# Sketch matrices as first loads, longer dummy matmuls, token-ordered q with interleaved projections, and a causal mask on row pairs

## The chip, the cores and the metric

The kernel runs on one core of one Trainium2 chip. The metric is the device time of one execution in microseconds (us), lower is better. TensorE (PE, with its weight loads as PEld), VectorE (DVE), ScalarE (ACT), GpSimd (POOL) and SyncE (SP) each run their own list of instructions in order; SP, and ACT in part, also issue the DMA transfers. They wait for one another through semaphores only.

## The reference

Two blocks follow each other. The first is a polynomial-sketch attention over 4 batches, 4 heads, 1088 tokens and 32 features; the second is a mixture of 4 attention experts, of which each token uses the best 2. S1 and S2 arrive as float64, all else as float32.

```
def phi(x):
    a = einsum('rd,bhsd->bhsr', S1, x)            # r = 8
    b = einsum('rd,bhsd->bhsr', S2, x)
    return einsum('bhsi,bhsj->bhsij', a, b)       # 64 features
q_p, k_p = phi(q), phi(k)
kv = einsum('bhsf,bhsd->bhfd', k_p, v);  z = k_p summed over tokens
x = (q_p @ kv) / (q_p @ z + 1e-6)                 # (B, S, H*D) = (4, 1088, 128)

logits = x @ w_gate;  topk = best 2 of 4;  w = softmax over those 2
for e in range(4):
    scores = (x @ wq[e]) @ (x @ wk[e]).T / 8, causal mask, softmax
    out += (weight of e, 0 if not chosen) * (softmax @ (x @ wv[e]) @ wo[e])
```

## The kernel before, in words

Nearly all of the work is matmuls and transposes on PE. PE's order is written out by hand (`manual_schedule`); a scheduler orders the other engines. Tokens lie in 9 tiles of 128 (the last has 64).

**Start.** SP loads k, then S1, q and v of batch 0 (`load`, L84); ACT loads wq, S2, wk, wv, w_gate and wo (L184 to L188). DVE turns the raw bits of S1 and S2 into float32 pairs (hi and lo, L128 to L147, some 20 small instructions), transposes them (`ST`, L153), and the block-diagonal sketch matrix `SKW` is filled from that by two copies on DVE and two on POOL (L155). Beforehand PE multiplies the identity with itself 10 times without use (`warm`, L552). Every float32 matmul has two records in the trace, and a float32 transpose one.

**prepare(b)** makes what the experts need of batch b: `begin` (L208) transposes k and q on DVE in 32x32 blocks; `sketch` (L220) multiplies with `SKW` (`kps`, `qps`), adds the lo part and forms the 64 products a feature row (`kp`, `qp`; DVE for batch 0, POOL later); `kvs` (L247) sums kv; `turn_features` (L263, `tq`) transposes qp; `numer` (L274, `num`) multiplies with kv, divides (`den`, `xs`); `turn_x` (L291, `tx`) transposes x into `xT`; `project` (L302, `qk`) makes q and k of the experts, `project_v` (L313, `vg`) v and the gate's logits, `gate` (L319) picks the two experts. q lies in the order in which its rows were loaded (34 tokens a partition), so `turn_x` puts its copy out of PSUM into token order with a stride of 34 elements.

For batch 0 the pieces run one after the other, and the projections of the first 1024 columns come when all of x is there. For batches 1 to 3 the same pieces are fillers: `spend` (L468) puts one between the units of the batch before, by a share of the costs that stand beside the pieces (L342 to L362).

**Units.** A unit is one tile of 128 queries and a pair of experts. `scores` (L367) multiplies on half of PE's rows each (64 features an expert: expert e on rows 64e to 64e+63, `sc`), adds the causal mask to the last 128 columns by a matmul of a 128x128 bfloat16 identity with a mask (L382, one per expert, on all 128 rows), DVE takes the maximum (L386, L389), ACT the exponential (L365). The scores are transposed (`tp`, L434), multiplied with v (`av`, L497) and wo (`po`, L540). There are 16 units a batch, 64 in all, and a last unit of 64 queries a batch (`scores_last`, L393) whose mask is at L412. `evacuate` (L67) copies PSUM to SBUF on ACT, each third time on DVE. PSUM has four buffers `tp` for all but the scores.

```
for e in range(2):
    nc.tensor.matmul(sc[e][:, 128 * i : n], identb, cmask, start=False, stop=True)
```

Of the kernel before, what the change touches and what calls it, by code (L numbers as in the profile page):

```python
# [19 lines left out]
def kernel(  # L20
# [20 lines left out]
    nc = tc.nc  # L41
# [59 lines left out]
    nc.vector.memset(raw, 0.0 if NS == 1 else 0)  # L101
    for x, s in enumerate((S1, S2)):
        eng = (nc.sync, nc.scalar)[x]
        if NS == 1:
            eng.dma_start(out=raw[R * x : R * x + R], in_=s)
        else:
            eng.dma_start(out=raw[R * x : R * x + R].rearrange("p d w -> p (d w)"), in_=s.bitcast(I32))
    load(0)
    if NS == 2:
# [34 lines left out]
        both(last, last, ok, ALU.mult)  # L144
# [23 lines left out]
    identb = const("identb", [128, 128], BF16)  # L168
    nc.vector.tensor_copy(identb, ident)
    cmask = const("cmask", [128, 128], BF16)  # L170
    make_causal_mask(nc, cmask, mask_val=-1e30)
# [8 lines left out]
    wqk = const("wqk", [128, 2, E, HD])  # L180
    wvg = const("wvg", [128, E * HD + E])
    wo_sb = const("wo", [128, NG, DM])
    for x, w in enumerate((wq, wk)):
        nc.scalar.dma_start(out=wqk[:, x], in_=w.rearrange("e p d -> p e d"))  # L184
    nc.scalar.dma_start(
        out=wvg[:, 0 : E * HD].rearrange("p (e d) -> p e d", e=E), in_=wv.rearrange("e p d -> p e d"))
    nc.scalar.dma_start(out=wvg[:, E * HD :], in_=w_gate)
    nc.scalar.dma_start(out=wo_sb, in_=wo.rearrange("(g e) h d -> (e h) g d", g=NG))  # L188

    nc.vector.tensor_scalar_mul(wqk[:, 0], wqk[:, 0], scale)  # L190


    def prepare(b):
# [13 lines left out]

        def begin():  # L208
# [3 lines left out]
            with tc.issue_after(mark[0]) if b < 2 else nullcontext():  # L212
# [3 lines left out]
                nc.vector.transpose(qT[:, 0:S], qin)  # L216
# [57 lines left out]
        def numer(g):  # L274
            num = bank(f"num{b}_{g}")
            for y in range(6):
                nc.tensor.matmul(num[:, 66 * y : 66 * y + 66], qpT[:, 6 * g + y],  # L277
                                 kvz[:, y % 2].rearrange("p h d -> p (h d)"), start=True, stop=True)
            nu = num[:, 0 : 12 * (D + 1)].rearrange("p (m d) -> p m d", d=D + 1)
            den = p2.tile([128, 12], F32, tag="den", name=f"den{b}_{g}")  # L280
            xs = p2.tile([128, 3, 128], F32, tag="xs", name=f"xs{b}_{g}", bufs=3)
            nc.vector.tensor_scalar_add(den, nu[:, :, D], 1e-6)
            nc.vector.reciprocal(den, den)
            last = nc.vector.tensor_tensor(
                out=xs.rearrange("p x (h d) -> p (x h) d", d=D), in0=nu[:, :, 0:D],
                in1=den[:, :, None].to_broadcast([128, 12, D]), op=ALU.mult)
            if first:
                mark[:] = [last.ins]
            xss[g] = xs

        def turn_x(g):  # L291
            tx = bank(f"tx{b}_{g}")
            for x in range(3):
                nc.tensor.transpose(tx[:, 128 * x : 128 * x + 128], xss[g][:, x], ident)
            c0, c1 = 12 * g, min(12 * g + 12, C)
            evacuate(xT.rearrange("p (t c) -> p c t", c=C)[:, c0:c1, :],
                     tx[:, 0 : 32 * (c1 - c0)].rearrange("p (c t) -> p c t", t=32))
# [21 lines left out]
        def gate():  # L319

            lg = vt[:, :, E * HD :]
            mine = lg[:, :, :, None].to_broadcast([128, NJ, E, E])
            theirs = lg[:, :, None, :].to_broadcast([128, NJ, E, E])
            gt = p2.tile([128, NJ, E, E], F32, tag="gt", name=f"gt{b}")
            eq = p2.tile([128, NJ, E, E], F32, tag="eq", name=f"eq{b}")
            rank = p2.tile([128, NJ, E], F32, tag="rank", name=f"rank{b}")
            top = p2.tile([128, NJ], F32, tag="top", name=f"top{b}")
            nc.vector.tensor_tensor(out=gt, in0=theirs, in1=mine, op=ALU.is_gt)
            nc.vector.tensor_tensor(out=eq, in0=theirs, in1=mine, op=ALU.is_equal)
            nc.vector.tensor_tensor(out=eq, in0=eq, in1=lower[:, None].to_broadcast([128, NJ, E, E]), op=ALU.mult)  # L330
# [3 lines left out]
            nc.vector.tensor_tensor(out=gw, in0=lg, in1=top[:, :, None].to_broadcast([128, NJ, E]), op=ALU.subtract)  # L334
            nc.scalar.activation(out=gw, in_=gw, func=ACTF.Exp)
            nc.vector.scalar_tensor_tensor(out=gw, in0=rank, scalar=2.0, in1=gw, op0=ALU.is_lt, op1=ALU.mult)
            nc.vector.reduce_sum(top, gw, axis=AX.X)
            nc.vector.tensor_scalar_add(top, top, 1e-9)
            nc.vector.reciprocal(top, top)
            nc.vector.tensor_tensor(out=gw, in0=gw, in1=top[:, :, None].to_broadcast([128, NJ, E]), op=ALU.mult)  # L340
            for g in range(NG):
                nc.vector.tensor_copy(gw8[64 * g : 64 * g + 64], gw[0:64, NJ - 1, 2 * g : 2 * g + 2])  # L342
# [309 lines left out]
```

## Time and profile before

| what | us |
|---|---|
| three runs: lowest, median, highest | 418.72, 419.71, 420.01 |
| the profiled execution, its own time | 420.57 |
| its span in the trace, first to last instruction | 418.7 |
| PE busy | 396.7 (95%) |
| DVE, ACT, POOL busy | 232.1, 224.9, 55.9 |

The profiled execution's span is 1.9 us shorter than its time, and its time is 0.9 us above the median of the runs. Busy PE time is not PE at its peak: matmul records overlap. A record's "us" in a timeline is from its start to its modelled end.

### The profile page before, as it was taken

To read this page: it belongs to the slowest core of one execution; us is meant where nothing else is said; L and a number is where in the kernel's file an instruction comes from. 1 tells how busy PE (TensorE), PEld (TensorE's weight loads), DVE (VectorE), ACT (ScalarE), POOL (GpSimd) and SP (SyncE) were. 2 spreads that over 40 slices of the span, in tenths; PEclk is the share of its full clock that TensorE was granted. 3 is DMA by queue.
4 is the path that set the end of the run, shared out by engine and by line. 5 is a ranking of instruction groups with operands and counts; after the bars stand their busy time and mean duration, and the time that the engine had idled before them with its cause. 6 is when DMAs were issued, how large, how long until landed. Compare 5 with 4: busy or idle time off the path is not lost.

```text
span 418.7 us, 8188 instructions
## 1 busy us (share of the span) xinstructions
PE 396.7 (95%) x3284; PEld 274.1 (65%) x3284; DVE 232.1 (55%) x496; ACT 224.9 (54%) x564; POOL 55.9 (13%) x84
## 2 busy tenths in 40 slices
PE   5989999999999999998999999999999998999995
PEld 5965777865666766775765776786666565576663
DVE  5775756754854464656447345556575545545552
ACT  1325565655546464555745555575455655455662
POOL 2200460000000361000000063000000000000110
PEclk9989999999999999999999999999999999999999
DMA  8631032000000000000000000000000000000000
GB/s 201 170 104 58 0 112 65 6 8 2 13 3 15 5 0 14 2 14 0 15 1 2 14 3 14 2 12 2 2 13 2 0 14 5 2 14 4 2 13 28
DMA packets 11351, 9.98 MB, mean 24 GB/s; under 512 B 3632, under 2 KB 10288, under 8 KB 11312
## 3 DMA queue, kind: packets, MB, share of 16 engines
q1 hardware_dynamic: 9296, 8.92, 7.5%
q10 hardware_dynamic: 2016, 0.53, 0.7%
q8 instruction: 26, 0.43, 0.4%
q14 instruction: 13, 0.11, 0.1%
HBM read 7.22 MB, written 2.23 MB: 23 GB/s over the span
## 4 chain that ended last, share of the span: by engine, by line
PE 80%; ACT 9%; DVE 6%; issue 3%; DMA 1%; POOL 0%; POOLq 0%; ACTq 0%; DVEq 0%
PE sc L379 18%; PE tp L434 15%; PE av L497 14%; PE qk L304 7%; ACT a L365 6%; PE sc L382 3%; PE po L540 3%; PE num L277 3%; PE kps L229 2%; PE vg L316 2%; PE kv L255 2%; PE av L526 2%; PE tq L268 2%; PE sc L402 2%; DVE mx L389 2%
## 5 line engine op out<-in xcount | busy, mean ns | idle before, releaser
L365 ACT ACTIVATE a<-sc,mx 128x1024 f32<-128x1024 f32 (+7 forms) x136 | 103.0, 762 | 86.7 <-DVE mx L389 48.2
L434 PE MATMUL tp<-ident,a 128*128 128x128 f32 (+1 forms) x648 | 95.1, 278 | 6.3 <-ACT a L365 4.8
L389 DVE TENSOR_REDUCE mx<-sc 128x1 f32<-128x640 f32 (+3 forms) x64 | 62.6, 1019 | 49.0 <-PE sc L382 49.0
L72 ACT COPY aT<-tp 128x512 f32<-128x512 f32 (+1 forms) x122 | 63.1, 539 | 45.6 <-PE tp L434 45.2
L434 PEld LDWEIGHTS tp<-ident,a 128*128 128x128 f32 (+1 forms) x648 | 71.3, 140 | 22.4 <-ACT a L365 9.7
L379 PE MATMUL sc<-qkT 64*128 64x512 f32 (+3 forms) x384 | 80.9, 518 | 0.8 <-ACT a L365 0.8
L497 PE MATMUL av<-aT,vt 128*64 128x256 f32 (+1 forms) x640 | 69.2, 363 | 0.0
L450 POOL TENSOR_TENSOR rb<-gw,r 128x256 f32<-128x256 f32 (+1 forms) x36 | 21.2, 589 | 322.9 <-DVE r L447 258.2
L497 PEld LDWEIGHTS av<-aT,vt 128*64 128x64 f32 x640 | 42.9, 137 | 21.7 <-issue 0.2
L379 PEld LDWEIGHTS sc<-qkT 64*128 64x128 f32 x384 | 32.2, 185 | 31.3 <-issue 26.2
L70 DVE COPY aT<-tp 128x512 f32<-128x512 f32 (+2 forms) x58 | 37.7, 652 | 16.2 <-PE tp L434 15.7
L386 DVE TENSOR_REDUCE mx<-sc 128x2 f32<-128x256 f32 (+3 forms) x32 | 26.2, 819 | 19.7 <-PE sc L382 19.7
L304 PE MATMUL qk<-xT,wqk 128*128 128x512 f32 x64 | 33.0, 633 | 1.0 <-ACT xT L72 0.9
L365 ACT ACTIVATION_READ_ACCUMULATOR a<-sc,mx 128x1 f32 x136 | 27.1, 199 | 0.0
L382 PEld LDWEIGHTS <-identb 128*128 128x128 bf16 x128 | 7.3, 97 | 28.1 <-issue 26.2
L316 PE MATMUL vg<-wvg,xT 128*128 128x260 f32 (+1 forms) x72 | 21.4, 396 | 1.1 <-DVE vt L70 0.5
L540 PE MATMUL po<-wo,yT 128*128 128x128 f32 (+1 forms) x144 | 20.5, 282 | 1.7 <-ACT aT L72 0.8
L499 DVE TENSOR_TENSOR yT<-av,rs 128x256 f32<-128x256 f32 x32 | 13.5, 422 | 13.9 <-PE av L497 13.7
L540 PEld LDWEIGHTS po<-wo,yT 128*128 128x128 f32 (+1 forms) x144 | 17.5, 185 | 3.5 <-ACT aT L72 1.1
L382 PE MATMUL sc<-cmask,identb 128*128 128x128 bf16 x128 | 18.3, 224 | 0.0
L304 PEld LDWEIGHTS qk<-xT,wqk 128*128 128x128 f32 x64 | 11.1, 199 | 10.2 <-issue 5.9
L277 PE MATMUL num<-kvz,qpT 128*128 128x66 f32 x144 | 17.4, 271 | 0.0
(118 smaller groups left out, 402.3 us busy)
## 6 DMA issues: line engine op xcount, KB each, us to landing
kin<-in_k_dram SPq DMA_DIRECT2D x4, 544.0 KB, 3.7
qin<-in_q_dram SPq DMA_DIRECT2D x4, 544.0 KB, 5.5
vin<-in_v_dram SPq DMA_DIRECT2D x16, 128.0 KB, 3.4
out_dram<-ob SPq DMA_DIRECT2D x16, 128.0 KB, 1.8
wqk<-in_moe_wq_dram ACTq DMA_DIRECT2D x1, 128.0 KB, 4.3
wqk<-in_moe_wk_dram ACTq DMA_DIRECT2D x1, 128.0 KB, 6.6
wvg<-in_moe_wv_dram ACTq DMA_DIRECT2D x1, 128.0 KB, 6.8
wo<-in_moe_wo_dram ACTq DMA_DIRECT2D x1, 128.0 KB, 6.0
```

Of the source, the lines that this page charges most:

```text
L70: nc.vector.tensor_copy(out_, in_)
L72: nc.scalar.copy(out_, in_)
L277: nc.tensor.matmul(num[:, 66 * y : 66 * y + 66], qpT[:, 6 * g + y], kvz[:, y % 2].rearrange("p h d -> p (h d)"), start=True, stop=True)
L304: nc.tensor.matmul(t, wt(a), xT[:, 512 * c : 512 * c + 512], start=True, stop=True)
L316: nc.tensor.matmul(t[0:m, 0 : E * HD + E], xT[:, 128 * j : 128 * j + m], wvg, start=True, stop=True)
L365: nc.scalar.activation(out=dst, in_=src, func=ACTF.Exp, bias=mx, accum_out=z)
L379: nc.tensor.matmul(sc[e][:, c0:c1], qk[rows, g, 128 * i : 128 * i + 128], qk[rows, NG + g, c0:c1], start=True, stop=(c1 < n))
L382: nc.tensor.matmul(sc[e][:, 128 * i : n], identb, cmask, start=False, stop=True)
L389: nc.vector.tensor_reduce(mx[:, e : e + 1], sc[e][:, 0:n], axis=AX.X, op=ALU.max, negate=True)
L434: nc.tensor.transpose(tp[0:nk, k - k0, :], ats[e][:, 128 * j : 128 * j + nk], ident)
L497: nc.tensor.matmul(av[HD * e : HD * e + HD, lo:256], vt[:, j, c : c + HD], aT[:, 2 * j + e, lo:256], start=(j == 0), stop=(j == 2 * p + 1))
L540: nc.tensor.matmul(po[0:nq, DM * x : DM * x + DM], yT[:, g, 128 * x : 128 * x + nq], wo_sb[:, g], start=(g == 0), stop=(g == NG - 1))
```

## The change

The scheduler's lines move; L numbers below are those of the changed kernel. In parts:

1. S1 is SP's first transfer and S2 is ACT's first and only one. `load(0)` follows S1 on SP, and the weights wq, wk, wv, w_gate and wo follow `load(0)` there. The scaling of wq goes from DVE to POOL, and one DVE instruction of the decoding (the product of `last` with `ok`) is left out. `SKW` is filled by two copies on DVE, one on ACT and one on POOL.
2. The dummy matmuls read a tile of zeros that DVE sets, not the identity, and there are 16.
3. q is transposed into token order by DVE, in two halves (`turn_q`), the output with a stride of 34 elements; `turn_x` copies without a stride. The second half, and the loads of the next batch, are a piece of their own (`begin_rest`).
4. In batch 0, x is made in four chunks (tiles 0-1, 2-3, 4-6, 7-8), and the four projections of columns 0 to 511 stand between the later chunks. The costs beside the pieces of later batches are a little different (a sketch of one tile 0.22, not 0.9).
5. The mask of a unit is four matmuls on half of PE's rows, two per expert, 64 columns each, with a picking matrix `mpick` and a mask `mrows` of 64 columns; POOL makes both. The last unit's mask is on half of the rows too.

```
+    idle = const("idle", [128, 128])
+    nc.vector.memset(idle, 0.0)
     for x, s in enumerate((S1, S2)):
         eng = (nc.sync, nc.scalar)[x]
...
+            ins = eng.dma_start(out=raw[R * x : R * x + R].rearrange("p d w -> p (d w)"), in_=s.bitcast(I32))
+        if x == 0:
+            landing = ins
+            with tc.issue_after(landing.ins):
+                load(0)
...
+    with tc.issue_after(landing.ins):
+        for x, w in enumerate((wq, wk)):
+            nc.sync.dma_start(out=wqk[:, x], in_=w.rearrange("e p d -> p e d"))
...
-        both(last, last, ok, ALU.mult)
...
     for h in range(H):
-        (nc.vector, nc.gpsimd)[h % 2].tensor_copy(
+        last = (nc.vector.tensor_copy, nc.scalar.copy, nc.gpsimd.tensor_copy, nc.vector.tensor_copy)[h](
             SKW[32 * h : 32 * h + 32, :, :, h, :], ST[:, :, 0 : 2 * R].rearrange("d n (x r) -> d n x r", x=2))
...
-    for x, w in enumerate((wq, wk)):
-        nc.scalar.dma_start(out=wqk[:, x], in_=w.rearrange("e p d -> p e d"))
...
-    nc.vector.tensor_scalar_mul(wqk[:, 0], wqk[:, 0], scale)
+    nc.gpsimd.tensor_scalar_mul(wqk[:, 0], wqk[:, 0], scale)
...
+        def turn_q(c0):
+            c = slice(c0, c0 + C // 2)
+            nc.vector.transpose(qT[:, 0:S].rearrange("p (t c) -> p c t", c=C)[:, c],
+                                qin.rearrange("p (c d) -> p c d", d=D)[:, c])
...
-            evacuate(xT.rearrange("p (t c) -> p c t", c=C)[:, c0:c1, :],
-                     tx[:, 0 : 32 * (c1 - c0)].rearrange("p (c t) -> p c t", t=32))
+            t1 = min(128 * x1, S)
+            evacuate(xT[:, 128 * x0 : t1], tx[:, 0 : t1 - 128 * x0])
...
+        cuts = ((0, 2), (2, 4), (4, 7), (7, NJ)) if first else ((0, 3), (3, 6), (6, NJ))
...
+            pieces += [kv] + tq[0:2] + nu[0:1] + tq[2:3] + nu[1:2] + tx[0:1] + tq[3:4] + tx[1:2]
+            pieces += nu[2:3] + pr[0][0:1] + tq[4:5] + pr[0][1:2] + tx[2:3] + nu[3:4] + pr[0][2:4] + tx[3:4]
...
-        for e in range(2):
-            nc.tensor.matmul(sc[e][:, 128 * i : n], identb, cmask, start=False, stop=True)
+        for half in range(2):
+            for e in range(2):
+                rows = slice(64 * e, 64 * e + 64)
+                c0 = 128 * i + 64 * half
+                nc.tensor.matmul(sc[e][:, c0 : c0 + 64], mpick[rows, half], mrows[rows], start=False, stop=(half == 1))
...
-        for _ in range(10):
-            nc.tensor.matmul(warm[:, 0:128], ident, ident, start=True, stop=True)
+        for _ in range(16):
+            nc.tensor.matmul(warm[:, 0:128], idle, idle, start=True, stop=True)
```

On DVE at the start of the program, the rows from the decoded sketch matrix (`ST`) to the first product of features, before:

```order
L153 STREAM_TRANSPOSE ST<-S_sum 32x64
L213 STREAM_TRANSPOSE kT<-kin 128x1024
L155 COPY SKW<-ST 32x4x8 x2
L215 STREAM_TRANSPOSE kT<-kin 128x64
L216 STREAM_TRANSPOSE qT<-qin 128x1088
L169 CAST identb<-ident 128x128
L235 TENSOR_TENSOR kab_191<-kab_191,kps_0_193 128x2x128
```

and in the changed kernel:

```order
L167 STREAM_TRANSPOSE ST<-S_sum 32x64
L169 COPY SKW<-ST 32x4x8 x2
L237 STREAM_TRANSPOSE kT<-kin 128x1024
L239 STREAM_TRANSPOSE kT<-kin 128x64
L229 STREAM_TRANSPOSE qT<-qin 128x17x32 x2
L263 TENSOR_TENSOR kab_207<-kab_207,kps_0_209 128x2x128
L267 TENSOR_TENSOR kp_208<-kab_207 128x1024
```

The copies into `SKW` now stand ahead of k's transpose, and q's transpose is two instructions. On ACT the list now begins with the load of S2, then the load of the activation table, which stands behind a wait for `ST`, then a copy into `SKW`.

On PE in batch 0, from the last transposes of x to the first scores, before:

```order
L268 MATMUL tq_16_324<-ident,qp_215 128x128 x2
L294 MATMUL tx_0_328<-ident,xs_0_302 128x128 x3
L277 MATMUL num_2_333<-kvz,qpT_177 128x66 x6
L294 MATMUL tx_1_345<-ident,xs_1_320 128x128 x3
L294 MATMUL tx_2_350<-ident,xs_2_341 128x128 x3
L304 MATMUL qk_0_0_355<-xT_173,wqk 128x512
L304 MATMUL qk_2_0_358<-xT_173,wqk 128x512
L304 MATMUL qk_1_0_361<-xT_173,wqk 128x512
L304 MATMUL qk_3_0_364<-xT_173,wqk 128x512
L379 MATMUL sc_0_0_375<-qkT_174 128x128 x2
```

and now:

```order
L306 MATMUL num_4_353<-kvz,qpT_201 128x66 x6
L332 MATMUL qk_0_0_365<-xT_197,wqk 128x512
L296 MATMUL tq_16_368<-ident,qp_240 128x128 x2
L332 MATMUL qk_2_0_372<-xT_197,wqk 128x512
L323 MATMUL tx_4_375<-ident,xs_4_361 128x128 x3
L306 MATMUL num_7_380<-kvz,qpT_201 128x66 x4
L332 MATMUL qk_1_0_390<-xT_197,wqk 128x512
L332 MATMUL qk_3_0_393<-xT_197,wqk 128x512
L323 MATMUL tx_7_396<-ident,xs_7_386 128x128 x2
L416 MATMUL sc_0_0_408<-qkT_198 128x128 x2
```

The projections, which stood behind the last transpose of x, now stand between the chunks of x.

On PE in the first unit of scores, before and now (the names after the arrow are the two operands):

```order
L379 MATMUL sc_0_0_375<-qkT_174 128x128 x2
L382 LDWEIGHTS identb
L382 MATMUL sc_0_0_375<-cmask,identb 128x128
L382 LDWEIGHTS identb
L382 MATMUL sc_0_0_375<-cmask,identb 128x128
L316 MATMUL vg_0_386<-wvg,xT_173 128x260
```

```order
L416 MATMUL sc_0_0_408<-qkT_198 128x128 x2
L422 LDWEIGHTS mpick
L422 MATMUL sc_0_0_408<-mrows,mpick 128x64
L422 LDWEIGHTS mpick
L422 MATMUL sc_0_0_408<-mrows,mpick 128x64
L422 LDWEIGHTS mpick
L422 MATMUL sc_0_0_408<-mrows,mpick 128x64
L422 LDWEIGHTS mpick
L422 MATMUL sc_0_0_408<-mrows,mpick 128x64
L344 MATMUL vg_0_421<-wvg,xT_197 128x260
```

Two weight loads and two matmuls of 128 columns on 128 rows have become four and four, of 64 columns on 64 rows. What follows the mask on PE is the same in kind in both kernels: in 32 of the 64 units a transpose `tp`, in 31 the product `av`, in one `vg`.

## Rows read from the trace of the kernel before

**Rows 1.** The page's part 4, the chain that ended last, by engine.
```profile
PE 80%; ACT 9%; DVE 6%; issue 3%; DMA 1%; POOL 0%; POOLq 0%; ACTq 0%; DVEq 0%
```

**Rows 2.** Busy time by stretch: length; PE, PEld, DVE, ACT, POOL; clock; DMA share, GB/s.
```profile
14.90:16.30 1.40, 1.39 (x13) 1.19 (x11) 1.40 (x2) 0.57 (x2) 0.00 (x0) 1.00 1.04 263
16.60:25.00 8.40, 8.32 (x126) 8.06 (x127) 7.31 (x15) 2.55 (x6) 1.60 (x2) 1.00 0.38 89
25.00:28.00 3.00, 1.39 (x11) 0.91 (x10) 2.91 (x7) 1.66 (x2) 0.00 (x0) 1.00 0.00 0
28.50:31.50 3.00, 3.00 (x5) 1.27 (x4) 1.23 (x2) 0.02 (x1) 0.00 (x0) 0.50 0.80 239
```

**Rows 3.** Timeline 0 to 32 us: start, length, engine, line, operation [idle before, releaser].
```profile
0.80 0.11 DVE L101 MEMSET S_raw<- 32x64 int32 x1 [0.80 <-PEq L636]
...
2.40 4.64 PE L552 MATMUL warm<-ident 128*128 128x128 f32 x20 [2.40 <-POOL ident masks.py:199]
...
5.10 0.29 DVE L190 TENSOR_SCALAR wqk<-wqk 128x256 f32<-128x256 f32 x1 [4.18 <-DMA wqk<-in_moe_wq_dram]
5.31 0.16 DVE L123 TENSOR_SCALAR S_ex<-S_raw 32x32 int32<-32x32 int32 x1
...
5.57 1.28 ACT L233 ACT_TABLE_LOAD   x1 [5.57 <-DVE S_ex L123]
...
7.76 0.23 DVE L153 STREAM_TRANSPOSE ST<-S_sum 32x64 f32<-32x64 f32 x1
7.93 1.19 DVE L213 STREAM_TRANSPOSE kT<-kin 128x1024 f32<-128x1024 f32 x1
...
9.52 4.18 PE L229 MATMUL kps<-SKW,kT 128*128 128x128 f32 x18 [2.49 <-POOL lower L175]
...
12.01 0.42 DVE L235 TENSOR_TENSOR kab<-kab,kps 128x256 f32<-128x256 f32 x1 [1.06 <-ACT kab L233]
...
13.71 0.42 DVE L235 TENSOR_TENSOR kab<-kab,kps 128x256 f32<-128x256 f32 x1 [1.29 <-ACT kab L233]
...
18.72 2.41 DVE L239 TENSOR_TENSOR qp<-qab 128x1024 f32<-128x1024 f32 x2
...
24.65 0.88 DVE L70 COPY xT<-tx 128x384 f32<-128x384 f32 x1
...
27.77 1.27 DVE L216 STREAM_TRANSPOSE qT<-qin 128x1088 f32<-128x1088 f32 x1
```

**Rows 4.** The chain of waits from 17 to 41 us, in order of time.
```profile
28.03 5.40 PE qk L304 x8
...
34.07 4.14 PE vg L316 x18
```

**Rows 5.** The page's part 6, DMA issues: count, size, median us to landing.
```profile
kin<-in_k_dram SPq DMA_DIRECT2D x4, 544.0 KB, 3.7
...
out_dram<-ob SPq DMA_DIRECT2D x4, 32.0 KB, 1.8
```

**Rows 6.** Timeline at 209 us: a mask that the product `av` follows.
```profile
209.86 1.02 PE L379 MATMUL sc<-qkT 64*128 64x512 f32 x4
...
210.82 0.28 PE L382 MATMUL sc<-cmask,identb 128*128 128x128 bf16 x2
...
211.03 0.44 PE L497 MATMUL av<-aT,vt 128*64 128x256 f32 x2
```

**Rows 7.** Timeline at 203 us: a mask that a transpose follows.
```profile
202.87 0.49 PE L379 MATMUL sc<-qkT 64*128 64x384 f32 x2
...
203.41 0.39 PE L434 MATMUL tp<-ident,a 128*128 128x128 f32 x2
```

**Rows 8.** Timeline at 122 us: the last unit, two groups that share PE's division.
```profile
121.59 0.61 PE L402 MATMUL sc<-qkT 64*64 64x512 f32 x4
122.02 0.29 PE L402 MATMUL ext<-qkT 64*64 64x64 f32 x8
```

**Rows 9.** The page's part 5, weight loads of the transposes of scores.
```profile
L434 PEld LDWEIGHTS tp<-ident,a 128*128 128x128 f32 (+1 forms) x648 | 71.3, 140 | 22.4 <-ACT a L365 9.7
```

More of the change, by code (lines that the diff above doesn't have):

```diff
@@ L8 @@
 from concourse._compat import with_exitstack
-from concourse.masks import make_causal_mask, make_identity
+from concourse.masks import make_identity
 F32 = mybir.dt.float32
@@ L167 @@
     make_identity(nc, ident)
[L168 to L171, printed above, removed]
+    mrows = const("mrows", [128, 64], BF16)
+    mpick = const("mpick", [128, 2, 128], BF16)
+    nc.gpsimd.memset(mrows, 0.0)
+    nc.gpsimd.memset(mpick, 0.0)
+    for e in range(2):
+        rows = slice(64 * e, 64 * e + 64)
+        for out_, cols, base, keep, fill in (
+            (mrows[rows], 64, 0, ALU.is_gt, -1e30),
+            (mpick[rows, 0], 128, -1, ALU.not_equal, 1.0),
+            (mpick[rows, 1, 64:], 64, -1, ALU.not_equal, 1.0)):
+            nc.gpsimd.affine_select(out=out_, in_=out_, compare_op=keep, fill=fill,
+                                    base=base, pattern=[[-1, cols]], channel_multiplier=1)
+        nc.gpsimd.memset(mpick[64 * e : 64 * e + 1, 1, 0:64], 1.0)
     lower = const("lower", [128, E, E])
@@ L215, in begin, with begin_rest @@
                 nc.vector.transpose(kT[:, 128 * n : S], kin[:, 128 * n : S])
-                nc.vector.transpose(qT[:, 0:S], qin)
+                turn_q(0)
+        def begin_rest():
+            with tc.issue_after(mark[0]) if b < 2 else nullcontext():
+                turn_q(C // 2)
             if b + 1 < B:
@@ L284, in numer, with turn_x @@
             last = nc.vector.tensor_tensor(
-                out=xs.rearrange("p x (h d) -> p (x h) d", d=D), in0=nu[:, :, 0:D],
-                in1=den[:, :, None].to_broadcast([128, 12, D]), op=ALU.mult)
-            if first:
+                out=xs[:, 0 : x1 - x0].rearrange("p x (h d) -> p (x h) d", d=D), in0=nu[:, :, 0:D],
+                in1=den[:, :, None].to_broadcast([128, m, D]), op=ALU.mult)
+            if first and x1 == NJ:
                 mark[:] = [last.ins]
[L289 to L295, printed above, removed]
-            evacuate(xT.rearrange("p (t c) -> p c t", c=C)[:, c0:c1, :],
-                     tx[:, 0 : 32 * (c1 - c0)].rearrange("p (c t) -> p c t", t=32))
+            xss[x0] = xs
+        def turn_x(x0, x1):
+            tx = bank(f"tx{b}_{x0}")
+            for x in range(x0, x1):
+                nc.tensor.transpose(tx[:, 128 * (x - x0) : 128 * (x - x0) + 128], xss[x0][:, x - x0], ident)
+            t1 = min(128 * x1, S)
+            evacuate(xT[:, 128 * x0 : t1], tx[:, 0 : t1 - 128 * x0])
         def wt(a):
@@ L352, in prepare @@
-        pieces = [(0.0, begin)] + sk["k"] + sk["q"] + [wait, (2.0, lambda: (kvs(0), kvs(1))), wait, wait]
-        pieces += tq[0:3] + nu[0:1] + tq[3:4] + nu[1:2] + tq[4:5] + tx[0:1] + nu[2:3] + tx[1:2] + [wait] + tx[2:3]
-        rest = pr[1] + [(0.5, project_tails)]
+            nc.vector.tensor_tensor(out=w, in0=w, in1=tops, op=ALU.mult)
+            if j1 == NJ:
+                for g in range(NG):
+                    nc.vector.tensor_copy(gw8[64 * g : 64 * g + 64], gw[0:64, NJ - 1, 2 * g : 2 * g + 2])
@@ new lines, in piece @@
+        def piece(us, f, *args):
+            return us, lambda: f(*args)
+        wait = (0.9, None)
+        kq = [[piece(0.22 * (min(j + NB, NJ) - j), sketch, nm, t, j) for j in range(0, NJ, NB)]
+              for nm, t in (("k", kT), ("q", qT))]
+        tq = [piece(0.5, turn_features, y) for y in range(0, 2 * NJ, 4)]
+        cuts = ((0, 2), (2, 4), (4, 7), (7, NJ)) if first else ((0, 3), (3, 6), (6, NJ))
+        nu, tx = ([piece(us * (x1 - x0), f, x0, x1) for x0, x1 in cuts] for us, f in ((0.43, numer), (0.12, turn_x)))
```

92 lines of the change are left out of this document (46 added, 46 removed).

## The prediction, made before the changed kernel ran

> **What bounds the kernel now.** I read the chain that ended last first, then the busy time by stretch, then the timeline of the start, then single masks. The chain is PE for 80% [rows 1]: from the first scores on, the kernel is a queue of matmuls with small holes, so what counts there is what a unit costs PE. The first 33 us are different. There PE waits for loads, for DVE, or runs at the lower of its two clock levels, and nothing else of the program can fill in, since no scores exist yet. Every microsecond by which the first scores come earlier is one off the end, as long as PE is kept fed afterwards. In the rows the chain reaches the first scores at 28.03 + 5.40 = 33.43 [rows 4]. So I count in two sums: how far that moment moves, and what a mask costs, 64 times.
>
> **The sketch matrix.** DVE's decoding starts at 5.31, behind a scaling of wq for which DVE sat idle 4.18 us [rows 3]; S1 and S2 are themselves queued behind k and wq. Now they are the first transfer of either queue. They still wait for the memset that ends at 0.91 [rows 3], so they issue at about 0.95. A small transfer with nothing ahead of it lands after 1.8 us, a k transfer after 3.7 [rows 5]; I take 1.8, since these are 2 KB, and keep 3.7 as the bound: landing at 2.8 (4.7). The decoding took 7.76 + 0.23 - 5.31 = 2.68; without one of its dependent instructions (0.11 by the average step of these some 20) it is 2.57, so ST is there at 5.4 instead of 7.99. Then two paths run side by side. DVE: two copies into SKW (0.3 is my estimate, from the 0.11 to 0.23 of the small instructions) and k's transpose, 1.19 [rows 3], to 6.9. ACT: the table load, 1.28, which lay idle at 5.57 before [rows 3], is now behind the wait for ST, and its copy follows: 6.9 too. **This is a new wait**, but it ends with k's transpose. The first sketch matmul can start at 7.0, not 9.52: 2.5 earlier. k lands at about 1.3 + 3.7 = 5.0, so it isn't late. The weights on SP's queue behind load(0) have until 20 us; what hides them is the whole feature stage. wq's scaling on POOL comes after the copies of v, and nobody waits for it before 20 us either. POOL's six selects and three more memsets for the mask lie before the copy of v, in time that POOL spent idle.
>
> **The clock at the start.** A dummy record took 4.64 / 20 = 0.232, the sketch records of k 4.18 / 18 = 0.232 [rows 3], and from 14.90 on 13 records took 1.40, or 0.11 [rows 2]: the slow pace is the 1.2 GHz level, the fast one 2.4. The clock column says 1.00 for the early stretches too, but the paces tell otherwise. So 4.64 us of dummies, followed by a hole to 9.52, did not raise the clock, and 5.4 us without a hole did (9.52 to 14.9). The other rise is after 28.0: at 0.50 until 31.5 at least [rows 2], fast by the end of that chain piece (33.43). The dummies now start at about 1.1, on a tile that DVE sets, and 16 make 32 records, 7.4 us at the slow pace. That is longer than either of the two stretches of work before a rise, so I take the clock to be up before the last third of them; they then end near 7.2, when the sketch may start. k's sketch then runs at 0.11 a record. Its first bank (8 records) takes 0.9, not 1.9, and the first DVE addition, 2.49 after the first matmul before (12.01 - 9.52), comes 1.5 after it: 8.7. By then q's transposes must be done: 6.9 + 0.2 + 1.27 = 8.4 if a strided output costs nothing, 9.6 at twice the time. The row that bounds this: a strided copy of 384 elements took 0.88, 2.3 ns an element, while q's transpose took 1.17 [rows 3]. I take 9.0.
>
> **Features on DVE.** From its first addition (12.01) to the last product of q (18.72 + 2.41 = 21.13) is 9.12, of which 1.29 was a wait for k's slow second bank [rows 3], which goes. 7.8 remain, so q's features are there at 16.8, not 21.1: 4.3 earlier. POOL's copy of v runs beside it in both.
>
> **From features to scores.** Before, this took 33.43 - 21.13 = 12.3: transposes, sums over kv, divisions, x, and then the projections in one block. From 25 to 28 PE worked 1.39 of 3.00, and after that the clock was at half: eight projection records took 5.40 [rows 2, 4]. At full pace they are 512 columns x 2 passes, 0.43 each (four passes over two row halves stand 0.43 apart [rows 8]), 3.4 in all, so 2.0 go if PE doesn't fall idle first. The interleaving fills the hole with them: the projections need only tiles 0 to 3 of x, and while DVE divides a later chunk PE projects. PE's own work from the first transposed feature to the scores is 18 + 36 + 9 records at 0.12 and 3.4, about 11; it can start when q's first product is there (about 14.5), and I add 1.2 for three divisions that are still waited for. That gives the first scores at 26.7, 6.7 earlier.
>
> **Given back.** DVE now has batch 1's transposes (1.2 + 0.2 + 1.27, up to 2.5 for a strided q) among its copies of the projections and of v, where they lay in the hole before. The v stage is 4.14 of PE [rows 4] through four PSUM buffers, a third of them emptied by DVE: I take 0.7 (0 to 2.5). **The start is worth 6.0**, between 3.0 (loads at the late bound, half of the clock gain) and 8.
>
> **The mask.** In a unit both experts stream at once on the two halves of PE's rows; 512 columns pass in 122.02 - 121.59 = 0.43, and a following group in the same division starts with no gap [rows 8]. Where av follows, the last pair begins at 209.86 + 0.43 = 210.29 and ends at 210.72; the mask, on all rows, starts 0.10 later, and av 0.21 after that: 0.31 from the last score to av [rows 6]. So each change of division costs about 0.10, and the old mask needs two of them ahead of av. Ahead of a transpose it needs one: 202.87 + 0.32 = 203.19, the transpose at 203.41, 0.22 [rows 7]. The new mask is in the scores' own division: two pairs of 64 columns, 0.03 each, plus up to 0.10 where the second pair's weights show, then one change, 0.10. Ahead of av that is 0.16 to 0.24, a gain of 0.07 to 0.15 in 31 units. Ahead of a transpose or vg it is 0.16 to 0.24 too, but their weights, which came in behind the old mask in the same division, now come after the change: 0 to 0.14 more [rows 9], so between 0.06 gained and 0.16 lost in 33 units. Middle: 31 x 0.11 - 33 x 0.05 = 1.8; PE is 80% of the chain, so **1.4**, between 6.6 gained and 3.1 lost. The Trainium skill (TensorEngine Tiling, Key Properties) says that changing the tiling mode drains TensorE, while a change of tile does not; the rows agree (0.10 against none). It also says (TensorE: Matmul & The Clock Gate, in the passage on 56 against 53.3 ns) that with hardware decode off a matmul costs the sequencer some 62 ns; as an estimate by that page, two more matmuls a unit would cost 0.12, and 64 units 8. Against it stand eight records in 0.29 [rows 8], so the sum goes without it; it has its place under the third rival.
>
> **The sum.** 6.0 + 1.4 = 7.4 off. The profiled execution took 420.6, so it would be 413.2; on the median of the runs, 0.9 lower, **412.3**. Other edits cost nothing I can see: x's copies without a stride save ACT and DVE a little in each batch, q's with a stride cost DVE about as much, and DVE is not the bound there. Fillers of batches 1 to 3 move by a place here and there; I allow 1.5 either way.
>
> **Rivals.** (a) The clock: it stays low through the dummies, or falls while PE waits for DVE between 11 and 21. The price is the one seen after 28 us, 2.0, plus the slower sketch, about 1: 415. For it: 4.64 us of dummies did nothing. Against: PE at 8.32 of 8.40 with transposes and short matmuls kept the clock up [rows 2]. (The Trainium skill, TensorE: Matmul & The Clock Gate, Part 4, says that transposes don't count as PE-busy for the clock; those rows, a good part of them transposes, show no fall.) (b) The start gains only half, because S lands like a k transfer, or because DVE and POOL disturb each other through v's copy: 415.5. For it: the last two products took 2.41, though the second has a quarter of the columns [rows 3]. (c) Slower: the four weight loads of a mask don't hide and the pairs run one after another, so that a unit costs PE 0.2 more: 64 x 0.2 = 12.8 against 6.0, 426.5. It decides from 6.0 / 64 = 0.094 a unit; at 0.12 a unit the kernel would be 1.7 slower than before, 421.4. Against it: weights that change between the two groups of [rows 8] without a gap. (0.12 is what the estimate from the page on the clock gate gives; I give it 0.02 of this rival's chance.) (d) The change does not do what it says: SP or ACT issues S no earlier in effect, and DVE is the bound throughout: 419. (e) The mask reaches its better bound: 408.
>
> **How the numbers follow.** Forecast 0.60, (a) 0.13, (b) 0.12, (c) 0.05, (d) 0.05, (e) 0.05. The range takes in the forecast with its own spread (409.5 to 415), and most of (a) and (b): 408.5 to 416.5; it leaves out (c), (d), part of (e) and the worst of (b), about 0.2. A difference of 0.3%, 1.3 us, is about what a measurement can tell from none. Faster 0.89: forecast, (a), (b) and (e) less a slip of 0.01. Same 0.06: (d) and a part of (c). Slower 0.05: the rest of (c) and that slip.
>
> **What would show it.** Right: S's decoding starts near 2.9; the sketch records of k stand 0.11 apart from the first; k's sketch at 7 to 8; projection records 0.43 apart at a granted clock of 1.00 with no stretch at 0.50 before 40 us; the first scores at 26 to 28; av 0.2 after the last score instead of 0.31. Wrong: first scores after 30, slow sketch records, a mask that ends later than before, or a gain at the first scores that is not there any more at 60 us, which would mean that DVE's load of copies and transposes is the new bound of that stage.

## The result and the profile after

The changed kernel took 409.01 us (median of 4 runs, 408.75 to 410.48), the kernel before 419.86 (418.72 to 420.60): a ratio of 0.9751, with a 95% interval of 0.9719 to 0.9783. That is 10.5 to 10.9 us off, where 7.4 were forecast; the time lies in the range (408.5 to 416.5), 3.3 below the forecast. The profiled execution took 408.94 with a span of 407.2, against 418.7 before.

One thing is needed to read what follows: executions of one kernel differ by 1 to 5 us, mostly with their mean granted clock (the changed kernel: 407.0 to 407.3 at 0.999, 408.6 at 0.994), so beside the medians I compare spans at 0.998 and above, where a kernel has them.

From the page of the changed kernel, the clock column:

```profile
PEclk9999999999999999999999999999999999999999
```

PE is 80% of the chain, as before [rows 1], and the stretch at the lower clock ahead of the first scores [rows 2] is gone. The start, from its timeline (0 to 22 us):

```profile
1.11 6.68 PE L593 MATMUL warm<-idle 128*128 128x128 f32 x32 [1.11 <-DVE idle L103]
...
2.63 0.17 DVE L138 TENSOR_SCALAR S_ex<-S_raw 32x32 int32<-32x32 int32 x1 [1.57 <-DMA S_raw<-in_S_dram]
...
7.63 2.17 PE L257 MATMUL kps<-SKW,kT 128*128 128x128 f32 x18
...
7.89 2.23 DVE L229 STREAM_TRANSPOSE qT<-qin 128x544 f32<-128x544 f32 x2 [0.68 <-DMA qin<-in_q_dram]
...
9.96 0.41 DVE L263 TENSOR_TENSOR kab<-kab,kps 128x256 f32<-128x256 f32 x1
10.09 1.06 POOL L233 COPY vp<-vin 128x1024 f32<-128x1024 f32 x1 [2.31 <-DMA vin<-in_v_dram]
...
10.41 1.81 DVE L267 TENSOR_TENSOR kp<-kab 128x1024 f32<-128x1024 f32 x1
...
17.25 0.43 DVE L267 TENSOR_TENSOR qp<-qab 128x256 f32<-128x256 f32 x1
```

The decoding starts 2.68 earlier than in [rows 3], the first addition 2.05 (9.96 for 12.01), the last product of q ends at 17.68 for 21.13. Then the scores of the first two units (timelines), now and before:

```profile
27.70 0.49 PE L416 MATMUL sc<-qkT 64*128 64x128 f32 x4
...
33.52 0.70 PE L416 MATMUL sc<-qkT 64*128 64x256 f32 x4
```

```profile
33.36 0.49 PE L379 MATMUL sc<-qkT 64*128 64x128 f32 x4
...
39.20 0.70 PE L379 MATMUL sc<-qkT 64*128 64x256 f32 x4
```

The first scores come at 27.70; by the chain of [rows 4] they came at 33.43, by their own record, which I use from here, at 33.36. That is 5.66 earlier. The second unit's scores start 5.68 earlier, at 33.52: the stage of v between them gave nothing back. From there on the lead grows mainly where a mask stands ahead of `av`: by 0.16 at each, to 6.67 at the sixteenth unit, late in batch 0. So two gains are seen this far, 5.7 at the start and 0.16 at each such mask. What batches 1 to 3 add to that and take from it stands at the end of the part on the prediction.

A mask ahead of `av`, and one ahead of a transpose, in the changed kernel (timeline, 55 and 60 us):

```profile
55.05 1.13 PE L416 MATMUL sc<-qkT 64*128 64x512 f32 x4
56.02 0.23 PE L422 MATMUL sc<-mrows,mpick 64*128 64x64 bf16 x4
56.17 0.87 PE L538 MATMUL av<-aT,vt 128*64 128x256 f32 x6
```

```profile
59.52 1.35 PE L416 MATMUL sc<-qkT 64*128 64x512 f32 x8
60.70 0.23 PE L422 MATMUL sc<-mrows,mpick 64*128 64x64 bf16 x4
60.85 0.66 PE L475 MATMUL tp<-ident,a 128*128 128x128 f32 x4
```

From the first score to the end of six records of `av` this is 56.17 + 0.87 - 55.05 = 1.99; to the end of four transposes 60.85 + 0.66 - 59.52 = 1.99. The next section sets the old mask and another beside them.

### The profile page after: what moved, and what is told of

Read it like the earlier page. It is cut to its first block, busy times and chain, and to the rows that moved or that the text cites. A ratio compares the mean times of both kernels' runs of the same rounds, so it can differ in the third digit from the quotient of the medians.

```text
span 407.2 us, 8480 instructions
## 1 busy us (share of the span) xinstructions
PE 388.0 (95%) x3424; PEld 278.3 (68%) x3424; DVE 231.6 (57%) x501; ACT 224.4 (55%) x566; POOL 58.8 (14%) x92
## 3 DMA queue, kind: packets, MB, share of 16 engines
HBM read 7.22 MB, written 2.23 MB: 23 GB/s over the span
## 4 chain that ended last, share of the span: by engine, by line
PE 80%; DVE 7%; ACT 7%; issue 2%; DMA 1%; POOLq 0%; SPq 0%; POOL 0%; ACTq 0%; DVEq 0%
PE sc L416 18%; PE tp L475 17%; PE av L538 14%; PE qk L332 7%; ACT a L402 5%; PE num L306 4%; PE vg L344 3%; PE po L581 3%; PE av L567 2%; PE sc L442 2%; PE kv L283 2%; PE kps L257 2%; PE qps L257 1%; DMA qin<-in_q_dram 1%; ACT aT L72 1%
## 5 line engine op out<-in xcount | busy, mean ns | idle before, releaser
L475 PE MATMUL tp<-ident,a 128*128 128x128 f32 (+1 forms) x648 | 96.3, 280 | 6.6 <-ACT a L402 4.6
L72 ACT COPY aT<-tp 128x512 f32<-128x512 f32 (+2 forms) x117 | 63.8, 559 | 51.3 <-PE tp L475 50.7
L332 PE MATMUL qk<-xT,wqk 128*128 128x512 f32 x64 | 31.7, 604 | 0.0
L422 PEld LDWEIGHTS <-mpick 64*128 64x128 bf16 x256 | 13.2, 94 | 17.0 <-issue 12.6
L72 ACT COPY qkT<-qk 128x512 f32<-128x512 f32 x24 | 14.0, 589 | 11.4 <-PE qk L332 11.4
L306 PEld LDWEIGHTS num<-kvz,qpT 128*128 128x128 f32 x144 | 17.1, 192 | 1.2 <-ACT qpT L72 0.5
```

The lines of the kernel that those rows point to most:

```text
L72: nc.scalar.copy(out_, in_)
L306: nc.tensor.matmul(num[:, 66 * (y - 2 * x0) : 66 * (y - 2 * x0) + 66], qpT[:, y], kvz[:, y % 2].rearrange("p h d -> p (h d)"), start=True, ...
L332: nc.tensor.matmul(t, wt(a), xT[:, 512 * c : 512 * c + 512], start=True, stop=True)
L475: nc.tensor.transpose(tp[0:nk, k - k0, :], ats[e][:, 128 * j : 128 * j + nk], ident)
```

## Experiments

**The mask: put back, alone, and in a third division.** Three kernels: the changed one with the old mask (`old_mask`), the one before with the new mask alone (`mask_alone`), and the changed one with the old mask cut by output columns, which puts it into the division of `av` (`mask_columns`, code abridged). The division is the part of PE's rows and columns that one matmul takes: 64*128 for the scores, 128*64 for `av`, 128*128 for the old mask and the transposes.

```diff
 for e in range(2):
-    matmul(sc[e][:, 128*i : n], identb, cmask, ...)
+    for c in range(2):
+        matmul(sc[e][64*c : 64*c+64, 128*i : n], identb[:, 64*c : 64*c+64], cmask, ...)
```

> The changed kernel with the old mask (one matmul of 128 rows and 128 columns for each expert), all else as changed. Theory M (the mask was undersized in the prediction: 0.16 us saved in each of 31 units that are followed by av, 0.02 to 0.07 in each of 33 others): 409.0 + 5.6 = 414.6 us (413.5 to 415.7). Theory P (mask as predicted, 1.4 us; the other 3 us of the gain come from the order of the work in batches 1 to 3 or from copies without a stride): 410.4 us (409.5 to 411.5).

> The kernel before with the new mask alone. Theory M: 419.9 - 5.6 = 414.3 us (413 to 415.5), and the first scores where they were, near 33.4. Theory P: 418.5 us (417.5 to 419.5). If start and mask depend on each other, the two single effects do not add up to 10.9.

> The changed kernel with a mask of 128 rows cut by output columns: two matmuls of 128 rows and 64 weight columns for each expert, which is the division that av uses, not that of the scores or of the transposes. Theory D (a mask's cost is its changes of division): ahead of av there is one change instead of the old mask's two, so av begins about 0.1 us sooner after the last score than with the old mask; ahead of a transpose there are two instead of one, so it begins about 0.1 us later; the total is near that of the old mask (413 to 416.5). Rival W (the old mask costs by its columns, its 128-row weights or the number of its matmuls, and division has no part): the same time from the last score to the next work whether av or a transpose follows, and both later than with the new mask.

Measured: with the old mask 416.30 us, ratio 0.9890 (0.9858 to 0.9923), 1.4% above the changed kernel's ratio, or 5.8 us; its spans at 0.998 are 412.3 and 412.5, so 5.2 more than 407.1. New mask alone: 414.50, ratio 0.9869 (0.9840 to 0.9898), so 5.5 off, with the first scores at 32.92, 0.4 from where they were. Columns: 415.54, ratio 0.9892 (0.9864 to 0.9921), spans of 413.5 to 413.8 at 0.998, so 1.2 above the old mask. Theory M holds, P falls. The single effects, 5.5 for the mask and 4.6 for all else (0.9890), make 10.1 of the 10.5 that the whole change gave by its ratio, so nothing shows that they depend on each other. (The old mask's median, above the range of M, has the clock's falls in it: four of its six executions ran at 0.992 to 0.994.) The same two places, with the old mask (timeline, 55 and 60 us):

```profile
54.94 1.13 PE L406 MATMUL sc<-qkT 64*128 64x512 f32 x4
56.00 0.28 PE L409 MATMUL sc<-cmask,identb 128*128 128x128 bf16 x2
56.22 0.87 PE L524 MATMUL av<-aT,vt 128*64 128x256 f32 x6
...
59.56 1.35 PE L406 MATMUL sc<-qkT 64*128 64x512 f32 x8
60.84 0.28 PE L409 MATMUL sc<-cmask,identb 128*128 128x128 bf16 x2
60.96 0.61 PE L461 MATMUL tp<-ident,a 128*128 128x128 f32 x4
```

and with the mask by columns (56 and 61 us):

```profile
55.84 1.13 PE L406 MATMUL sc<-qkT 64*128 64x512 f32 x4
56.90 0.30 PE L410 MATMUL sc<-cmask,identb 128*64 128x128 bf16 x4
57.04 0.82 PE L526 MATMUL av<-aT,vt 128*64 128x256 f32 x6
...
60.33 1.35 PE L406 MATMUL sc<-qkT 64*128 64x512 f32 x8
61.61 0.30 PE L410 MATMUL sc<-cmask,identb 128*64 128x128 bf16 x4
61.84 0.66 PE L463 MATMUL tp<-ident,a 128*128 128x128 f32 x4
```

| First score to the end of | old mask | by columns | new mask |
|---|---|---|---|
| six `av` records | 2.15 | 2.02 | 1.99 |
| four transposes | 2.01 | 2.17 | 1.99 |

A mask is cheap where it shares its division with a neighbour: by columns it saves 0.13 ahead of `av` and loses 0.16 ahead of a transpose, and 33 x 0.16 - 31 x 0.13 = 1.2, the measured difference. That is theory D; W, by which the next work would not matter, falls. The new mask saves 0.160 in each of 31 units and, by the single records, 0.016 in each of 33: 5.5 us.

**The dummies: ten instead of sixteen** (`for _ in range(10)`).

> The changed kernel with 10 dummy matmuls instead of 16, so that they end near 5.7 and PE idles until the sketch at 7.6. Theory C (the raised clock at the sketch was worth its share of the predicted 6.0): k's sketch at 0.23 us a record, 4.2 us long, first scores 1 to 2 us later, 410 to 411. Theory V (DVE is the bound from its first addition to the last feature, and a slow first bank of 1.9 us is ready before q's transposes end near 10.1): sketch as slow, but the first addition still near 10.0 to 10.4 and the total 409.0 to 409.6.

Measured: 410.35 us, ratio 0.9747 (0.9718 to 0.9776), the changed kernel's to within 0.0004; its best span is 406.8. The start of the ten-dummy run (timeline), and the clock there (windows: length, PE busy, granted clock, DMA share, GB/s):

```profile
7.15 3.37 PE L257 MATMUL kps<-SKW,kT 128*128 128x128 f32 x18 [1.88 <-DVE kT L239]
...
9.86 0.41 DVE L263 TENSOR_TENSOR kab<-kab,kps 128x256 f32<-128x256 f32 x1
...
27.65 0.49 PE L416 MATMUL sc<-qkT 64*128 64x128 f32 x4
```

```profile
8.00:10.00 2.00, 2.00 (x12) 0.51 0.94 186
```

The clock stood low over both sketches, that of k took 3.37 instead of 2.17, and the first scores come at 27.65 all the same: theory V. (The median lies in C's range, but three of the six executions ran at 0.989 or 0.990, and the profiled one has a fall that the changed kernel's lacks, late, in the fourth batch: 0.55 from 356 to 358 us.) The longer dummies even hold the sketch back, since PE is at them until 7.6 while k's transposes are done at 7.2 in the changed kernel.

**The loads: S behind k and the weights again** (no `issue_after` for `load(0)`, the weights on ACT's queue, wq's scaling on DVE).

> The changed kernel with the loads as before: S1 behind k and S2 behind wq on their queues, the weights on ACT's queue, wq's scaling on DVE ahead of the decoding. Theory S (the path from S to the first DVE addition carries the gain of the start): decoding from about 5.3, first addition about 2.5 later than the changed kernel's 9.96, first scores 30.2, total 411.5 us (411 to 412). Rival Q (in the changed kernel q's transposes waited 0.68 us for q, which lands earlier beside a later S): first addition only 1.5 to 2 us later, first scores 29.3 to 29.7, total 410.7. Rival D (DVE's later work or the v stage takes the loss up): total 409 to 409.6.

Measured: 411.86 us, ratio 0.9800 (0.9764 to 0.9835), 0.5% above the changed kernel's ratio. Its start (timeline), and its clock:

```profile
10.08 4.18 PE L254 MATMUL kps<-SKW,kT 128*128 128x128 f32 x18 [2.85 <-DVE kT L236]
...
12.56 0.42 DVE L260 TENSOR_TENSOR kab<-kab,kps 128x256 f32<-128x256 f32 x1 [0.41 <-ACT kab L258]
```

```profile
10.00:12.00 2.00, 1.92 (x9) 0.50 0.75 160
```

The decoding starts at 5.62 and the first addition is 2.6 later, as theory S has it, and the first scores come at 31.02, 3.3 later: 0.8 more than S says in this execution. PE had idled 2.85 us behind the dummies, the clock was at 0.50, and k's sketch took 4.18. Here q had landed, its transposes were done sooner, and DVE waited for the slow sketch (0.41); in the run with ten dummies it did not.

**The order: projections in a block, and the old order of q.** `block_order` takes x in three pieces and all projections behind them; `strided_x` also gives q its old token order back, so that the copies of x have the stride again (abridged):

```diff
-evacuate(xT[:, 128*x0 : t1], tx[...])
+evacuate(xT.rearrange("p (t c) -> p c t", c=C)[:, c0:c1, :], tx[...])
```

> The changed kernel with batch 0 in the old order: x in three pieces of three tiles, all four projections in a block behind the last piece. Theory C (the order spares a fall of the clock, as predicted): a stretch at a granted clock of 0.50 while the projections run, first scores 3 us later, 30.5 to 31, total 411.5 to 412. Theory O (no fall of the clock here, since PE's holes are shorter than in the kernel before; the interleaving only fills PE's waits for the divisions): clock 1.00 throughout, first scores 1 to 1.8 us later, total 410 to 410.8. Rival D (later work takes it up): 409 to 409.6.

> The run with the block order, with q again in its old order: one q transpose without a stride, and x put into token order by strided copies. So batch 0 is that of the kernel before from q's features on, behind the new loads and dummies, with the new mask. Theory T (it was the strided copies of x, 0.88 us against 0.55, that opened the holes of PE and let the clock fall before the projections in the kernel before): two holes of PE near 23 to 25, a stretch at a granted clock of 0.50 over the projections, first scores 1.5 to 2.5 us later than the block order's 27.87, total 409 to 410. Rival N (the fall came from the late and slow start, not from the copies): clock 1.00, first scores 28.0 to 28.5, total 407.3 to 408. The copies of batches 1 to 3 have a stride here too and add 0 to 0.5.

Measured: the block order 407.39 us, ratio 0.9692 (0.9666 to 0.9718), below the changed kernel; the old order of q on top of it 407.17, ratio 0.9699 (0.9672 to 0.9726). First the block order (timeline), then the old order of q (timeline and windows):

```profile
23.21 0.48 ACT L72 COPY xT<-tx 128x384 f32<-128x384 f32 x1 [1.58 <-PE tx L323]
...
24.34 3.60 PE L332 MATMUL qk<-xT,wqk 128*128 128x512 f32 x8
...
27.87 0.49 PE L416 MATMUL sc<-qkT 64*128 64x128 f32 x4
```

```profile
7.81 1.31 DVE L229 STREAM_TRANSPOSE qT<-qin 128x1088 f32<-128x1088 f32 x1 [0.71 <-DMA qin<-in_q_dram]
...
9.04 0.38 DVE L262 TENSOR_TENSOR kab<-kab,kps 128x256 f32<-128x256 f32 x1
...
22.14 0.89 ACT L72 COPY xT<-tx 128x384 f32<-128x384 f32 x1 [1.58 <-PE tx L322]
...
24.39 5.37 PE L332 MATMUL qk<-xT,wqk 128*128 128x512 f32 x8 [0.95 <-ACT xT L72]
...
29.68 0.49 PE L416 MATMUL sc<-qkT 64*128 64x128 f32 x4
```

```profile
26.00:28.00 2.00, 2.00 (x3) 0.50 0.95 285
```

The block order has no fall of the clock, and its first scores are 0.17 later, not 1 to 3, in an execution in which q itself landed 0.40 later (its transposes start at 8.29, not 7.89). Counted from there, the first scores take 19.58, and 19.81 in the changed kernel. So the interleaving is worth nothing that can be seen. (Among executions whose start is the same, q's landing moves the first scores by some 0.3 either way: 27.47 and 28.02 in two runs below.) The total missed all three expectations. With the strided copies, 0.89 us on ACT where the same tile takes 0.48 without a stride, there are two holes of PE, 0.79 and 0.95, the clock falls, and the projections take 5.37 instead of 3.60, as in [rows 4]: the mechanism of theory T, in this execution. Its total did not follow: the first addition is 0.9 earlier, since q's transpose without a stride takes 1.31 and not 2.23, and the better executions ran at 404.6 to 404.9. Two of the six had a mean clock of 1.000, so the same copies do not always bring a fall.

**Who copies.** Every third copy out of PSUM goes to DVE, by a counter. The changed kernel makes four copies of x in batch 0 where three were made before, which moves the counter by one for all that follows. `rotate2` and `rotate1` move it on by two and by one behind batch 0's pieces (`turn[0] += 2`).

> The changed kernel, where the counter that gives every third copy out of PSUM to DVE is moved on by two once batch 0's features and projections are issued. From there on each copy goes to the engine to which it goes in the run with the block order; batch 0 up to the first scores is untouched. Theory R (the block order's gain of 1.5 us lies in who copies what after the first scores, not in batch 0's order): first scores at 27.7 as in the changed kernel, span 405.5 to 406 against 407.2, time 407.2 to 407.8. Rival O (it lies in batch 0's order itself): span 406.8 to 407.4, time 408.6 to 409.2.

> The same with the counter moved on by one, the third of the three rotations. Theory R: another time than both, by which mark is open; between 407 and 411 us, with other waits of PE ahead of its transposes in batches 1 to 3. Rival O: span 406.8 to 407.4, time 408.6 to 409.2, as the changed kernel.

Measured: by two 407.89 us, ratio 0.9707 (0.9682 to 0.9731), spans of 405.4 to 406.1 at 0.998 and above; by one 409.17, ratio 0.9751 (0.9725 to 0.9776), 407.1 to 407.4. PE's waits in the changed kernel, then in the one moved by two (waited for; us in total, times, longest):

```profile
PE tp L475 <- ACT aT L72: 1.3, 2, 0.9
PE vg L344 <- ACT aT L72: 1.0, 2, 0.8
...
PE vg L344 <- ACT vt L72: 0.7, 2, 0.3
```

```profile
PE vg L344 <- ACT aT L72: 0.3, 2, 0.2
PE tp L475 <- DVE aT L70: 0.3, 1, 0.3
```

The first number is the sum and the second the count: six waits for ACT's copies, 3.0 us together, shrink to two, 0.3 together, with one of 0.3 for a copy of DVE's, and the waits for the exponentials grow from 4.6 to 5.4. (`po` waits 0.7 for a copy in both, for DVE's in the first and ACT's in the second.) What is left, 3.0 - 0.6 - 0.8 = 1.6, is the difference of the lowest spans. That is theory R, with a median 0.1 above its range: the block order's gain lies here and not in batch 0. The third rotation tells nothing apart: its 409.17 fits both theories.

**DVE at the start.** `fold_start` lets PE add the two halves of the sketch matrix; `fold_vact` also puts batch 0's copy of v on ACT (abridged):

```diff
-matmul(t[:, 128 columns], kT tile, SKW both halves, start=True, stop=True)
+matmul(t[:, 64 columns], kT tile, SKW[:, 0], start=True, stop=False)
+matmul(t[:, 64 columns], kT tile, SKW[:, 1], start=False, stop=True)
```

> The changed kernel, where in batch 0 PE adds the two halves of the sketch matrix itself: two matmuls of 64 columns into the same PSUM columns in place of one of 128 columns and a DVE addition. Theory V (DVE is the bound from its first addition to the last feature of q): the additions of 0.41, 0.54, 0.74 and 0.21 us are gone, q's last feature 1.5 to 1.9 us earlier than 17.68, first scores 26.0 to 26.4 instead of 27.7, total 407.3 to 407.8. Rival K (ACT's copies, PE's longer sketch of 36 short matmuls or the wait for v take DVE's place): first scores 27.2 to 27.8, total 408.6 to 409.2.

> As the run with PE's own addition, and batch 0's copy of v on ACT between the copies of k's and of q's sketches, instead of on POOL. Theory B (POOL's copy slows DVE's first feature product beside it, 1.81 us against 1.2 for the others): the first product takes 1.2 to 1.3, first scores another 0.5 us earlier, total 406.8 to 407.4. Rival A (the copy of v, some 1.2 us, now stands ahead of q's copies on ACT and delays q's products): the first product as fast, but the first scores where they were in the run with PE's addition alone or up to 0.6 later.

Measured: 412.30 us, ratio 0.9807 (0.9780 to 0.9833), and 412.70, ratio 0.9802 (0.9770 to 0.9834): both slower than the changed kernel. From the timeline of the first:

```profile
7.71 4.13 PE L259 MATMUL kps<-SKW,kT 128*128 128x64 f32 x36
...
10.18 1.21 DVE L270 TENSOR_TENSOR kp<-kab 128x1024 f32<-128x1024 f32 x1
10.34 1.95 POOL L233 COPY vp<-vin 128x1024 f32<-128x1024 f32 x1 [2.46 <-DMA vin<-in_v_dram]
...
29.65 0.49 PE L419 MATMUL sc<-qkT 64*128 64x128 f32 x4
```

36 records of 64 columns take 0.115 each, 18 of 128 columns 0.121: half the columns save nothing, and PE's sketch becomes the bound. Rival K, and worse than it said: the first scores are 1.95 later. The second run can't judge theory B: the first product of k takes 1.21 in both, with POOL's copy of v beside it here and without it there. Its first scores are 0.55 earlier (29.10), but its sketch started 0.62 and q's transposes 0.38 earlier. What decides, in these profiles, is who starts first. In the changed kernel POOL's copy began at 10.09, ahead of the product, and took 1.06, the product 1.81; here the product began first and took 1.21, the copy 1.95.

**A version that beats both.** `best` is the block order with v's copy on ACT and 14 dummies.

> The run with the block order, with batch 0's copy of v on ACT between the copies of k's and q's sketches instead of on POOL, and 14 dummies instead of 16. Theory B (POOL's copy slows DVE's first feature product, 1.81 us against 1.2; the first sketch waits for k's transposes near 7.1 and not for PE): first sketch near 7.2, first feature product 1.2 to 1.3, first scores 27.1 to 27.4, total 406.6 to 407.1. Rival A (the copy of v on ACT delays q's products or the sums over kv): first scores 27.8 to 28.5, total 407.3 to 408.2.

Measured: 406.87 us (406.66 to 408.09), ratio 0.9692 (0.9666 to 0.9718); the interval ends just below that of the changed kernel, 0.9719 to 0.9783. Its start (timeline):

```profile
10.15 1.23 DVE L270 TENSOR_TENSOR kp<-kab 128x1024 f32<-128x1024 f32 x1
...
26.89 0.49 PE L419 MATMUL sc<-qkT 64*128 64x128 f32 x4
```

The sketch starts at 7.12, the first product takes 1.23, and the first scores come 0.98 earlier than in the block order: theory B, and 0.2 ahead of its range. But 0.65 of that is q's earlier landing (7.64 for 8.29), and the product's 0.3 is what the edit bought (it took 1.53 in the block order). Against that kernel the ratio is the same and the lowest spans are 404.9 and 405.4, so what it adds to the block order is not shown.

## Why the prediction was right, and which term was too small

- **The sketch matrix.** Decoding at 2.63 (2.9 said), the table load behind ST and beside k's transpose, as said; the first sketch at 7.63 and not 7.0 to 7.2, held by the dummies, which costs nothing.
- **The clock at the start.** k's sketch ran at 0.12 a record, for 0.11 said. That it matters there was wrong: in the run with ten dummies the slow sketch lies beside q's transposes. It matters where q has landed, as with the late loads.
- **The first addition.** 9.96 for 9.0. The sum let q's transposes start at 7.1 (6.9 + 0.2) and gave them 1.9, half way between no cost and twice the time. They started at 7.89 and took 2.23. So 0.8 of the miss is the landing of q, for which DVE waited 0.68 and which the sum left out, and 0.3 is the stride, whose price the copies of x had already shown [rows 3]. The page of the kernel before had q's time to landing, longer than the 3.7 of k; issued at 1.83, q would have been due at 7.3 (the line below). In the six profiles that share the loads, the strided q and the interleaving (the changed kernel, its two runs with other masks, ten dummies, both rotations), the first scores come 19.8 to 20.0 behind the start of q's transposes (7.27 to 8.22). Without a stride the addition started at 9.04.

```profile
qin<-in_q_dram SPq DMA_DIRECT2D x4, 544.0 KB, 5.5
```

- **Features on DVE.** 17.68 - 9.96 = 7.72, for 7.8.
- **From features to scores.** 10.02, for 9.9, for the wrong reason. The interleaving gave nothing. The copies of x have no stride, so that one of the two holes ahead of the projections goes, and the clock stayed up; that the hole alone decides it is not shown, since it can stay up with the strided copies too.
- **Given back.** Nothing, for 0.7. The start is worth 5.7, for 6.0; two misses of about 1 us, late q features and no give-back, cancel, which is luck.
- **The mask** is the term that was mis-sized: 1.4 said, 5.5 measured. Three things in "Middle: 31 x 0.11 - 33 x 0.05 = 1.8; PE is 80% of the chain" were too careful. Ahead of `av` I left up to 0.10 for the second pair's weights; the second pair starts 0.028 behind the first, and the gain is 0.160, above my better bound of 0.15. Ahead of a transpose I took a loss of 0.05, since its weights would show; if they do, it is by less than the mask gains, and 0.016 is left. And a share of the chain seems to be no discount on a queue of matmuls: the new mask alone gave 5.5 of 5.5, though its interval, 4.3 to 6.7, does not quite exclude four fifths. (The upper end of the new mask, 0.24, is a slip for 0.06 + 0.10 + 0.10 = 0.26, which would have made the term 0.9.) Rival (e) had the size, 6.6 at most. (The Trainium skill, TensorEngine Tiling, Key Properties, says that a change of the tiling mode drains TensorE; the mask by columns agrees and gives the price, 0.13 to 0.16 a change here.)
- **Other edits, 0 with 1.5 either way.** Not nothing: the copy counter moved, which cost 1.1 (medians) to 1.8 (ratios), 1.6 by the lowest spans.
- **The rivals.** (a) did not come about in the profiled execution. (b) had a true part, POOL beside DVE's first product, worth 0.6 there, but the start gained nearly whole. (c) fell: the unit got shorter. (d) fell with the decoding at 2.63.

Start and mask, 5.7 + 5.5 = 11.2, stand against a span shorter by 11.5, but the copy counter's loss of 1.1 to 1.8 is in that span too. So 1.4 to 2.1 us of gain has no name. Most of it lies in batch 1: from its first scores to those of batch 2 the profiled executions took 101.35 before (127.64 to 228.99) and 98.44 now (120.81 to 219.25), at a granted clock of 1.00 in both, and 8 masks ahead of `av` and 8 ahead of a transpose explain 1.4 of these 2.91. The run with the mask by columns has that gain too: 100.13, though its masks cost 0.2 more there than the old ones. The fillers of that batch have other costs beside them and one piece more; no run puts the old ones back. Part of the rest may lie in the profiled execution of the kernel before: its executions in the experiments' runs spread from 416.9 to 420.0 in span. The cause stays open.

## What to carry to other kernels

Price a small matmul by the divisions of its neighbours: put it into the division of what comes before or after, and count every change before the columns. At a start that one engine bounds, give every load that it waits for a time of landing, cost each new access pattern on it from the nearest strided row, and don't pay for speed on engines that wait for it. When an edit changes the number of calls to something that takes turns, look at who gets which turn afterwards.

## What the hardware showed that I had not expected

- The same 128 x 128 mask, cut in two ways, costs 0.13 less or 0.16 more by what follows it.
- A sketch record of 64 columns takes 0.115 us, one of 128 columns 0.121, where each has its own weights.
- DVE's transpose of 128 x 1088 took 1.31 us, two of 128 x 544 with a stride 2.23.
- Between DVE's feature product and POOL's copy of v the one that starts first keeps its pace and the other is slowed. POOL first: copy 1.05 to 1.06, product 1.53 to 2.01 (six kernels' profiles). DVE first: product 1.21 to 1.23, copy 1.54 to 2.03 (three). In the changed kernel the copy ends at 11.15, and the product takes 1.07 from there. So these two engines can hold each other up without a semaphore. (The Trainium skill, SBUF — State Buffer, SBUF: two separate sides, says that the port pair that these two engines share goes to the one that starts first, for its whole instruction, and that the other waits; it holds among others where DVE's instruction has two inputs in SBUF, as this product has. These rows agree.)
- The clock falls after holes that need not be long, and not in every execution. In the run with the old order of q, 0.79 and 0.95 with little work between came ahead of a fall to 0.50 that made eight projections 1.77 longer; two of its six executions had a mean clock of 1.000. The changed kernel's profiled execution had PE idle 0.94 and 0.67 near 183 us without a fall; with the old mask, 1.04 and 0.67 at the same place were followed by one.
